# Retention feeding a SwiGLU block on one core: later retention with a row half per head, sequence and token half, 24 groups of small matmuls in place of 36, and a new order of steps

## The chip, the core and the metric

The kernel runs on one core of one Trainium2 chip. The metric is the device time in microseconds of that core, from launch to end. The kernel before takes 642.07 us (median of 3 runs, 642.02 to 642.96); lower is better. Times from the profile come from one profiled execution with a span of 640.5 us from its first to its last instruction.

The engines go by these names: PE is TensorE (PEld is its weight load), DVE is VectorE, ACT is ScalarE, POOL is GpSimd, SP is SyncE, which only issues transfers here. Each engine works through its own queue in the order in which the program issues instructions.

## What is computed

Retention over 4 sequences, 8 heads, 768 tokens and head size 64, then a SwiGLU feed-forward block over the 3072 tokens, all in float32:

```python
gamma = 1.0 - 2.0 ** (-5.0 - np.arange(H))
for t in range(S):
    state = gamma[None, :, None, None] * state + np.einsum('bhd,bhe->bhde', k[:, :, t], v[:, :, t])
    y[:, :, t] = scale * np.einsum('bhd,bhde->bhe', q[:, :, t], state)
...
x = y.transpose(0, 2, 1, 3).reshape(B * S, H * D)          # 3072 x 512
g = x @ w_gate                                             # 512 x 1536
silu = g * (1.0 / (1.0 + np.exp(-g)))
return silu * (x @ w_val) @ w_out                          # 1536 x 512
```

The retention is done in chunks. Within a chunk, scores (keys against queries) are weighted by a decay mask and multiplied with the values; what earlier tokens left is kept in a 64 x 64 state per head, read by the queries (scaled by the decay), decayed once per chunk, and increased by keys (scaled) against values.

## The kernel before

**Segments.** The 3072 tokens are worked in four segments of 768: two sequences of 384 tokens each. The feed-forward block of a segment has an up stage (12 column blocks of the gate and value weights; in the later segments each is 7 products of 128 x 128 blocks, `product` at L1088) and a down stage (12 steps f, each with six token blocks of 128, `down` at L1157, called D{f}.{tok}; three matmuls of 128x512 each, into banks 0 to 5 of PSUM). Numbers are kept exact by splitting each operand into three parts (`near_a/b/c` and `far_a/b/c`, L991 to L1007); the parts of the hidden values are made by h{f}.0 (ACT), h{f}.1 and h{f}.2 (DVE, 128x768 each). In the first segment the down weights are split too: d{f}.0 (ACT), d{f}.1 (POOL, 128x512), d{f}.2 (DVE, 128x512).

**Mixed stages.** The retention of the next segment is worked inside the down stage of the one before, so there are three mixed stages, each with three chunk positions p of two sequences, in token halves z of 64. PE does it in small matmuls of 64 x 64 (`mm`, L789; each leaves two records in the trace), set between D steps. Per p the kernel before has four groups: `s` (scores of both halves, 32 matmuls, `scores_of` L799), `A` (values of half 0, the old state's part, and the state's growth: `mix_a`, up to 40), `B` (`mix_b`, 32) and `C` (`mix_c`, 24): 12 groups in a stage, 36 in all.

**What stands around the groups.** dec{p}.{i} (`decayed`, L809, DVE) multiplies scores out of PSUM by the mask; q{p}.{i} (`scale_q2`, L814) scales the queries in place, one 128x512 on DVE and one on POOL; k{p}.{i} (`scale_k2`, L818) scales keys, 8 instructions of 128x64 on ACT (one of the six on POOL); was{p}.{z} (`decay2`, L885) decays the state, 4 instructions of 128x128 on ACT; new{p}.{z} (`keep_state`, L890, DVE) adds the growth out of PSUM; y{p}.{z}{j} (`bring_y`, L1020) copies the outputs out of PSUM, 16 copies of 64x128 per p on ACT. Then sum{p}.{m} and x{p}.{n}.{k} (`sum_x`, `x_part`) on DVE and ACT make the split operands of the next up stage. Scores of the first p stand in banks 4 and 5, those of the other two in banks 6 and 7, where the outputs and the state's growth stand as well.

**Order.** The order of all this on every engine is written out by hand as the text `PLAN` (L51): one name after another, and each name issues its instructions when its turn comes. `at(t, key, ...)` only registers what a name does; where PLAN has the name, its time t has no effect. l{n} are the loads of keys, queries, values and keys by rows (`load_pair`, L775: one or two transfers per chunk), L{f} and W{f} the loads of the weights, e{tok} and its store the output.

## Time and profile before

| what | us |
|---|---|
| median of the runs shown | 642.07 |
| span of the profiled execution | 640.5 |
| first mixed stage, from 127 to 196: DVE busy, ACT busy, POOL busy | 63.8, 50.2, 26.7 of 69 |
| second mixed stage, from 283 to 350: DVE, ACT, POOL | 50.1, 46.3, 10.0 of 67 |
| third mixed stage, from 435 to 502: DVE, ACT, POOL | 52.9, 44.7, 10.2 of 67 |
| ACT: copies of the outputs (L1022), decay of the state (L888), scaling of the keys (L824) | 36.6, 19.1, 29.8 in all |
| granted TensorE clock in all 40 slices | 0.9 or more |

A line of a timeline is: start, duration, engine, line of the kernel, operation, written tile <- read tiles, shape, number of instructions, and in brackets the idle time before it. An instruction on DVE is shown for about 0.07 us longer than it keeps the next one from starting. A line of the chain of waits is: start, length, engine and line, number of instructions. The windows give the busy time of each engine within a stretch.

### The profile page before, as it was taken

The page shows a single profiled execution, that of the slowest core. Times are in us where ns is not written, and L with a number is a line of the kernel's source. Part 1 is how long each engine was busy: PE and PEld are TensorE (multiplying, and loading weights), DVE is VectorE, ACT ScalarE, POOL GpSimd, SP SyncE. Part 2 cuts the span into 40 slices and gives each one's busy share as a digit, 9 for nine tenths or more (in the row PEclk, how much of TensorE's full clock was granted, in tenths as well). Part 3 has the DMA queues.
Part 4 walks back from the last instruction along what each step waited for, and adds up shares of the span by engine and source line. Part 5 has one row for each costly group of instructions (what it writes and reads, how often), then busy time and mean ns, then how long its engine had stood idle before and what let it go on. Part 6 is the DMA issues. An engine that isn't in the chain of part 4 may idle for free.

```text
span 640.5 us, 14132 instructions
## 1 busy us (share of the span) xinstructions
PE 632.9 (99%) x5587; PEld 580.4 (91%) x5587; DVE 484.1 (76%) x715; ACT 394.3 (62%) x868; POOL 261.1 (41%) x172
## 2 busy tenths in 40 slices
PE   7999999999999999999999999999999999999997
PEld 6899999987779999997778999998777999999886
DVE  4998787899898887665797869575789866768361
ACT  4787797777865565566766555564785555654221
POOL 1534445544425866630003665550101666663000
PEclk9999999999999999999999999999999999999999
DMA  9899998798787445258765640457776444304564
GB/s 320 291 332 326 376 329 269 268 326 305 266 285 278 168 148 173 75 179 260 247 239 214 211 152 15 175 196 246 226 258 248 154 164 173 116 1 151 194 214 148
DMA packets 50626, 139.60 MB, mean 218 GB/s; under 512 B 5120, under 2 KB 18176, under 8 KB 50560
## 3 DMA queue, kind: packets, MB, share of 16 engines
q1 hardware_dynamic: 49984, 137.92, 62.6%
q8 instruction: 44, 0.72, 0.5%
q10 hardware_dynamic: 576, 0.79, 0.3%
q14 instruction: 22, 0.18, 0.1%
HBM read 108.80 MB, written 29.88 MB: 217 GB/s over the span
## 4 chain that ended last, share of the span: by engine, by line
PE 97%; DMA 3%; SPq 0%; DVE 0%; ACT 0%; issue 0%
PE bank L1088 41%; PE bank L1157 32%; PE bank L919 13%; PE bank L789 6%; PE bank L937 3%; DMA hT<-in_v_n_dram 2%; PE bank L744 1%; DMA hT<-in_q_t_dram 1%; PE bank L730 0%; PE bank L715 0%; PE bank L633 0%; DVE chunk_x L1178 0%; SPq L513 0%; ACT chunk_x L1180 0%; SPq L466 0%
## 5 line engine op out<-in xcount | busy, mean ns | idle before, releaser
L1157 PE MATMUL bank<-oitem,gitem 128*128 128x512 f32 x867 | 208.2, 394 | 0.0
L1157 PEld LDWEIGHTS bank<-oitem,gitem 128*128 128x128 f32 x867 | 159.6, 188 | 34.5 <-DVE tmp L812 0.4
L997 POOL TENSOR_TENSOR gitem<-gitem 128x768 fp32r<-128x768 f32 x71 | 138.7, 1963 | 117.9 <-DVE gitem L994 99.0
L1088 PE MATMUL bank<-xa,gitem 128*128 128x384 f32 x864 | 160.5, 334 | 0.0
L1088 PEld LDWEIGHTS bank<-xa,gitem 128*128 128x128 f32 x864 | 150.8, 188 | 0.2
L997 POOL TENSOR_TENSOR oitem<-oitem 128x256 fp32r<-128x256 f32 (+1 forms) x60 | 64.1, 1074 | 56.8 <-DVE oitem L994 48.3
L1088 PE MATMUL bank<-xb,gitem 128*128 128x384 f32 x432 | 84.5, 334 | 0.0
L919 PE MATMUL bank<-xa,oitem 128*128 128x384 f32 x480 | 84.3, 335 | 0.0
L919 PEld LDWEIGHTS bank<-xa,oitem 128*128 128x128 f32 x480 | 83.0, 188 | 0.4 <-ACT tmp L444 0.2
L994 DVE SCALAR_TENSOR_TENSOR gitem<-gitem,loads 128x768 fp32r<-128x768 f32 x72 | 75.1, 1057 | 9.1 <-ACT gitem L991 7.5
L1088 PEld LDWEIGHTS bank<-xb,gitem 128*128 128x128 f32 x432 | 75.9, 188 | 0.4
L991 ACT ACTIVATE gitem<-loads 128x768 fp32r<-128x768 f32 x72 | 59.6, 843 | 26.0 <-PE bank L1088 16.8
L994 DVE SCALAR_TENSOR_TENSOR gitem<-gitem,hT 128x768 fp32r<-128x768 f32 x48 | 46.1, 965 | 24.4 <-ACT gitem L991 24.4
L991 ACT ACTIVATE gitem<-hT 128x768 fp32r<-128x768 f32 x48 | 40.2, 842 | 31.4 <-PE bank L1157 29.4
L1022 ACT COPY chunk_x<-bank 64x128 f32<-64x128 f32 x144 | 36.6, 260 | 32.6 <-PE bank L789 21.3
L401 DVE SCALAR_TENSOR_TENSOR gitem<-gitem 128x768 fp32r<-128x768 f32 x49 | 49.7, 1022 | 1.3 <-DVE gitem L994 0.5
L816 POOL TENSOR_TENSOR loads<-loads,tab 128x512 f32<-128x512 f32 x9 | 13.4, 1493 | 82.1 <-PE bank L789 44.6
L1088 PE MATMUL bank<-xb,oitem 128*128 128x384 f32 x216 | 43.4, 335 | 0.0
L1088 PEld LDWEIGHTS bank<-xb,oitem 128*128 128x128 f32 x216 | 37.9, 188 | 0.3
L994 DVE SCALAR_TENSOR_TENSOR oitem<-oitem,loads 128x256 fp32r<-128x256 f32 (+1 forms) x42 | 34.5, 824 | 2.1 <-ACT oitem L991 2.1
L1105 DVE TENSOR_TENSOR hT<-bank,tmp 128x384 f32<-128x384 f32 x36 | 20.0, 555 | 20.7 <-PE bank L1088 20.4
L1103 ACT COPY tmp<-bank 128x384 f32<-128x384 f32 x36 | 17.2, 478 | 28.3 <-PE bank L1088 19.3
(118 smaller groups left out, 789.8 us busy)
## 6 DMA issues: line engine op xcount, KB each, us to landing
loads<-wup SPq DMA_DIRECT2D x36, 896.0 KB, 4.7
oitem<-wdnt SPq DMA_DIRECT2D x33, 768.0 KB, 4.4
wdnt<-oitem SPq DMA_DIRECT2D x12, 768.0 KB, 5.5
wup<-first SPq DMA_DIRECT2D x9, 896.0 KB, 6.7
rawp<-in_w_gate_dram SPq DMA_DIRECT2D x12, 512.0 KB, 6.8
rawp<-in_w_val_dram SPq DMA_DIRECT2D x12, 512.0 KB, 6.2
rawp<-in_w_out_dram SPq DMA_DIRECT2D x12, 512.0 KB, 5.7
out_dram<-chunk_x SPq DMA_DIRECT2D x21, 256.0 KB, 2.1
```

What stands on the lines that cost most here:

```text
L401: stt(o, x, 1.0, y, op0=mul, op1=op)
L789: nc.tensor.matmul(o, a, b, start=start, stop=True, skip_group_check=True)
L919: nc.tensor.matmul(o, w[:, a, ts(b, P)], X0[:, a, i, NC - 1 - b], start=a == b == 0, stop=a == 2 and b == NC - 1, skip_group_check=True)
L937: nc.tensor.matmul(o, w[:, a, ts(b, P)], X0[:, a, :, NC - 1 - b, ts(j, P)], start=a == b == 0, stop=a == 2 and b == NC - 1, skip_group_che ...
L991: act(o[0], x, AF.Copy, scale=CUT / FAR)
L994: stt(o[1], f32(o[0]), -FAR, x, op0=mul, op1=add)
L997: op(o[2], f32(o[0]), f32(o[1]), op=add)
L1022: copy(cx[half[i], ds(2 * h, 2), c, half[z]], y.rearrange("p (b t) -> p b t", b=2))
L1088: nc.tensor.matmul(o, w[:, a, k], x[:, a, KH - 1 - k], start=start and a == k == 0, stop=a == 2 and k == KH - 1, skip_group_check=True)
L1103: steps = (lambda: copy(p1, x), lambda: tt(c11, z, p1, op=add), lambda: act(gate, c11, AF.Silu, scale=ONE), lambda: copy(u2, x), lambda: c ...
L1105: lambda: copy(p5, wb), lambda: tt(h1, x, p5, op=add),
L1157: nc.tensor.matmul(banks[tok][:, cols], hs[f][:, a, ds(i * TH + u * P, P)], wo[f][:, a, cols], start=f == a == 0, stop=f == NF - 1 and a = ...
```

## The change

**What it does.** The retention of the three mixed stages is laid out anew. The work is still 128 small matmuls per p, but the 128 rows of SBUF are assigned otherwise: a row half (64 partitions) belongs to a head pair, a sequence and a token half, by `row(z, c, g)`. With this the old state's part of both sequences can be worked together, and per p there are three groups (`s`, `A`, `B`), the last two by `mix2`. In PLAN the scores of the second p stand directly behind `A` of the first, so that a stage has 8 changeovers from D steps to small matmuls, and the three stages 24 (36 before).

**Banks.** The scores of the first and the second p stand in banks 4 and 5, those of the third in 6 and 7; D0.4 and D0.5 come behind `sc1`.

**What stands around the groups.** Scores are weighted by four DVE instructions per p (two of 128x384, two of 128x128). The queries are scaled by eight instructions of 64 partitions x 256 per p, four on DVE and four on POOL, and are written into the buffer of the keys, behind the scores that read it. The state is decayed by four instructions of 64 x 256 per p and z, all on POOL (`WAS_POOL`). Keys are scaled on ACT alone: 4 instructions of 128x128 and 8 of 128x64 per p. Outputs are copied by 4 instructions of 128x256 per p on ACT. Before the first mixed stage's parts, eight copies (`turn_state`, cv) put the state into the new layout.

**Loads.** Values and keys by rows come in four transfers of 64 partitions x 2 x 256 elements per pair (three before). Two pairs have new places (`chunk_x`, `tmp` and `last`). The first three loads of the first mixed stage, which were P2, P1 and P0 within the first up stage, come later, next to l3. The output's store is a step of its own, o{tok}.

**Order.** PLAN is written anew from the end of the first up stage on. PE's order in the second mixed stage, before and after (sc, A, B, C without their stage, p11.n and p0.n are products of the up stages):

```
-sc0 D0.0 p11.6 D0.2 D0.1 D0.4 D0.3 D1.0 D1.1 D0.5 A0 D1.5 D1.3 D2.1 B0 D1.2 D1.4 D2.5 D2.0 D2.3 D2.2 C0 ...
+sc0 p9.4 ... p11.6 D0.0 D0.1 D0.2 D0.3 A0 sc1 D1.0 D1.1 D1.2 D0.4 D0.5 D1.3 D1.5 D1.4 B0 D2.0 ... D3.1 A1
+D3.2 ... D4.3 B1 D4.5 ... D5.4 sc2 D6.0 ... D7.1 A2 D7.2 ... D8.3 B2 D8.4 ... D11.5 p0.0
```

In the first mixed stage W11:1 (the last product of the first up stage) is followed by sc0, D0.0 to D1.1, A0, sc1, and so on; ten D steps stand from D11.0 on to the next up stage. Two parts of PLAN there, with the names of DVE and POOL among PE's:

```
+    0/D4.5 1/y1.11 1/new1.1 0/d6.0 1/was2.03 0/D4.4 1/L0 0/h7.0 0/d6.1 0/D5.0 0/W7 1/y1.10 0/D5.1
+    0/h7.1 0/h8.0 1/was2.02 0/D5.2 1/x1.2.0 0/d6.2 1/was2.00 1/x1.1.0 0/D5.3 0/h7.2 0/Z6 1/was2.01 0/D5.4
...
+    1/sum2.0 0/Z10 0/d11.0 1/sum2.1 0/D9.5 1/w0.0.1 0/d11.1 0/D9.4 1/sum2.2 1/w0.1.0 0/D10.0 1/sum2.3 1/x2.0.0
+    0/d11.2 0/D10.1 1/w0.0.2 0/Z11 0/D11.0 1/w0.2.0 1/x2.1.2 0/D11.1 1/x2.1.1 0/D10.2 1/w0.1.1 0/e0 0/D11.2
```

In the up stages the products of one column block now follow each other in order (p5.0 to p5.6, then p6.0), where before two blocks were interleaved. The code, cut to its core (the removed functions are shown above):

```diff
+LATE = [(0.1, 'g4'), (14.2, 'g5'), (33.6, 'L'), (47.2, 'h0'), (47.2, 'h1'), (47.6, 'k4'), (53.1, 'k5'), (53.2, 'h2'), (56.3, 't4 t5')]
...
+    spots += [chunk_x[:, ts(i, 512)] for i in (2, 3)] + [tmp[:, ts(2, 512)], last]
+    HOME = (2, 3, 4, 5, 0, 1, 3, 6, 1, 4, 5, 0)
     blocks = [loads[:, ds(i, UNIT)] for i in (2048, 2048 + UNIT, 0)]
...
+    lmask = [local[:, ds(k * NP * HC, NP * HC)].rearrange("p (i n) -> p i n", i=2)
+             for k in range(2)]
+    lk, lg = (local[:, ds(2 * NP * HC + k * H, H)] for k in range(2))
+    lk = lk.rearrange("p (k n) -> p k n", k=2)
...
+    def row(z, c, g):
+
+        return g ^ (c & z & 1)
+
     def local_k():
 
         for m in range(2):
...
+            for k in range(2):
+                nc.sync.dma_start(out=lk[half[m], k],
+                                  in_=decays[half[1], ds(KDEC0 + NP * (k ^ m), NP)])
+        nc.sync.dma_start(out=lg, in_=decays[ds(D - 1, 1), ds(KDEC0, H)].to_broadcast([P, H]))
...
+            if w < 2:
+                nc.sync.dma_start(out=own[c], in_=src)
+                continue
+            for r in range(2):
+                step = D * DM + (c and 256 * (1 - 2 * r))
+                nc.sync.dma_start(out=two_of(own[c][half[r]]),
+                                  in_=bass.AP(src.tensor, src.offset + 256 * r,
+                                              [[DM, D], [step, 2], [1, 256]]))
...
     def scores_of(p, own):
...
+        scored[p] = own
         kt, qt = ([pairs(t) for t in given[p][w]] for w in range(2))
+        for z in range(2):
+            for b in range(2):
+                for c in range(2):
+                    for g in range(2):
+                        for i in range(2):
+                            mm(banks[own + i][half[row(z, c, g)], ds(256 * c + 128 * z + HC * b, HC)],
+                               kt[c][half[i], 2 * g + b, half[z]],
+                               qt[c][half[i], 2 * g + b, half[z]], z == b == c == 0)
+
+    def decayed(p, i, k):
+        if (p, i) not in att:
+            att[p, i] = (tmp if p % 2 else spare)[:, ts(i, 512)]
+        src = banks[scored[p] + i]
+        if k:
+            tt(att[p, i][:, 384:], src[:, 384:], lmask[1][:, i], op=mul)
+        else:
+            o, x = (t[:, :384].rearrange("p (a n) -> p a n", a=3) for t in (att[p, i], src))
+            tt(o, x, lmask[0][:, i][:, None, :].to_broadcast([P, 3, 128]), op=mul)
+
+    def scale_q2(p, c, i, r, op):
+
+        o = given[p][0][c][half[r], ts(i, 256)]
+        q, d = (pairs(t)[half[i]] if t is not qdec else t[half[i]]
+                for t in (given[p][1][c], qdec))
+        if c == 0:
+            op(o.rearrange("p (b t) -> p b t", b=2), q[:, ds(2 * r, 2)], d[:, ds(2 * r, 2)], op=mul)
+            return
+        x = []
+        for t in (q, d):
+            x.append(bass.AP(t.tensor, t.offset + HC * r, [list(t.ap[0]), [256 + HC * (1 - 2 * r), 2],
+                                                          [P, 2], [1, HC]]))
+        op(o.rearrange("p (g b t) -> p g b t", g=2, b=2), *x, op=mul)
+
+    def q_of(p, z, c, g, b, i):
+        r = row(z, c, g)
+        at = 256 * i + (256 // 2 * b + HC * z if c == 0 else 128 * g + HC * b)
+        return given[p][0][c][half[r], ds(at, HC)]
+
+    def scale_k2(p, c):
+        kd = given[p][3][c].rearrange("p (z n d) -> p z n d", z=2, n=NP)
         for n in range(NP):
...
+            if c == 0:
+                act(kd[:, :, n], kd[:, :, n], AF.Copy, scale=lk[:, 0, ds(n, 1)])
+            else:
+                for z in range(2):
+                    act(kd[:, z, n], kd[:, z, n], AF.Copy, scale=lk[:, z, ds(n, 1)])
...
+    def state_of2(z, c, g):
+
+        return states[half[row(z + 1, c, g)], z, row(z, c, g)]
+
+    def turn_state(i, g):
+
+        for c in range(2):
+            copy(state_of2(1, c, g).rearrange("p (b i) e -> p b i e", b=2)[:, :, i],
+                 states[half[i], 0, c, ds(2 * g, 2)])
+
+    def y_at(z, c, g, b, i):
+        return banks[R0 + row(z, c, g)][half[i], ds(256 * z + 128 * (g if z else c) + HC * b, HC)]
 
     def low(p, z):
...
+        for b in range(2):
+            for c in range(2):
+                for i in range(2):
                     for r in range(2):
...
+                        g = row(z, c, r)
+                        mm(y_at(z, c, g, b, i),
+                           given[p][2][c][half[r], ds(256 * z + D * (2 * b + i), D)],
+                           att[p, i][half[r], ds(256 * c + 128 * z + HC * b, HC)], b == c == 0)
+
+    def old(p, z):
         for b in range(2):
...
+            for c in range(2):
+                for i in range(2):
+                    for r in range(2):
+                        g = row(z, c, r)
+                        mm(y_at(z, c, g, b, i), state_of2(1 - z, c, g)[:, 2 * b + i],
+                           q_of(p, z, c, g, b, i))
 
     def grow(p, z):
         for n in range(NP):
...
+            for c in range(2):
+                for g in range(2):
+                    r, own = row(z, c, g), ds(256 * z + D * n, D)
+                    mm(banks[R0 + r][half[row(z + 1, c, g)], ds(256 * (1 - z) + D * n, D)],
+                       given[p][3][c][half[r], own], given[p][2][c][half[r], own])
+
+    def mix2(s, p, z):
+        low(p, z)
+        if has_old(s, p, z):
+            old(p, z)
+        if has_new(s, p, z):
+            grow(p, z)
+
+    def decay2(z, c, g, op):
+        r = row(z, c, g)
+        op(state_of2(z, c, g), state_of2(1 - z, c, g),
+           lg[half[r], ds(NP * g, NP)][:, :, None].to_broadcast([D, NP, D]), op=mul)
 
     def keep_state(s, p, z):
         for r in range(2):
...
+            new, st = states[:, z, r], banks[R0 + r][:, ds(256 * (1 - z), 256)]
+            st = st.rearrange("p (n e) -> p n e", n=NP)
             if has_old(s, p, z):
...
+    def bring_y(z, r):
+        y = banks[R0 + r][:, ts(z, 256)].rearrange("p (w b t) -> p w b t", w=2, b=2)
+        at, step = (HC + P * r, 512 + P * (1 - 2 * r)) if z else (512 * r, P)
+        copy(bass.AP(chunk_x.tensor, chunk_x.offset + at,
+                     [list(chunk_x.ap[0]), [step, 2], [256, 2], [1, HC]]), y)
...
+    def store(s, tok):
+        if (s, tok) in stored:
+            to, t = stored.pop((s, tok))
+            nc.sync.dma_start(out=to, in_=t)
...
+    Q_POOL, WAS_POOL = (1, 2, 5, 6), (0, 1, 2, 3)
...
+            for p in range(L):
+                at(t, f"{nxt}/sc{p}", scores_of, p, 6 if p == 2 else 4)
+                for i in range(4):
+                    at(t, f"{nxt}/dec{p}.{i}", decayed, p, i % 2, i // 2)
+                for i in range(8):
+                    at(t, f"{nxt}/q{p}.{i}", scale_q2, p, i // 4, i // 2 % 2, i % 2,
+                       pool if i in Q_POOL else tt)
+                for c in range(2):
+                    at(t, f"{nxt}/k{p}.{c}", scale_k2, p, c)
+                for z in range(2):
+                    at(t, f"{nxt}/{'AB'[z]}{p}", mix2, nxt, p, z)
+                    if has_new(nxt, p, z):
+                        for i in range(4 if has_old(nxt, p, z) else 0):
+                            at(t, f"{nxt}/was{p}.{z}{i}", decay2, z, i // 2, i % 2,
+                               pool if i in WAS_POOL else tt)
+                        at(t, f"{nxt}/new{p}.{z}", keep_state, nxt, p, z)
+                    for r in range(2):
+                        at(t, f"{nxt}/y{p}.{z}{r}", bring_y, z, r)
+                make_x(t, nxt, p, table)
```

More of the change, by code (lines that the diff above doesn't have):

```diff
@@ L224 @@
[L224 to L228 removed]
+    A0 I0 l0:0 l1:0 A2 A1 U0:0 s0 a0:1 r1 l0:2 s1 b0:1
@@ L1239, in down_stage @@
                 at(t + WHEN["end" if nxt else "last"][tok], f"{s}/e{tok}", finish, s, tok)
+                at(t + WHEN["end" if nxt else "last"][tok], f"{s}/o{tok}", store, s, tok)
         for f in range(NF):
@@ L1276, in tile_retnet_swiglu @@
     end = T0 + (NF - NPF) * UP0
-    for n in range(3, 5):
-        at(end + 0.1 + 0.01 * n, f"1/l{n}", load_pair, 1, n)
     t = down_stage(0, end)
@@ L1285, in tile_retnet_swiglu @@
         t += NF * UPT
-        if s + 1 < NSEG:
-            for n in range(5):
-                at(t - (18, 13, 12, 5, 4)[n], f"{s + 1}/l{n}", load_pair, s + 1, n)
         t = down_stage(s, t)
```

502 lines of the change are left out of this document (199 added, 303 removed).

## The prediction

> **What bounds the kernel now.** I read the chain of waits first: who sets the end.
>
> ```profile
> PE 97%; DMA 3%; SPq 0%; DVE 0%; ACT 0%; issue 0%
> ```
>
> From 18 us on PE waits for nobody. Whatever the change moves between ACT, DVE and POOL gains nothing by itself; only PE time counts, or a wait where there was none. So next, the chain in order of time, for what a group of small matmuls costs PE.
>
> ```profile
> 185.48 0.39 PE bank L789 x16
> 185.87 10.43 PE bank L1157 x45
> ...
> 291.64 2.27 PE bank L1157 x9
> 293.91 0.86 PE bank L789 x48
> 294.77 4.31 PE bank L1157 x18
> ...
> 305.61 1.09 PE bank L789 x64
> ```
>
> Two straight lines lie in these rows. Down matmuls: 45 take 10.43 and 9 take 2.27, so 0.2267 each (0.68 for a D step of three) and 0.23 over for each piece behind a group. Small matmuls: 64 records take 1.09 and 16 take 0.39, so 0.0146 each (0.0148 with the other rows) and 0.15 over. One changeover to small matmuls and back costs 0.15 + 0.23 = 0.38 us, besides the records.
>
> Then how near DVE and POOL are to becoming the bound. The tightest place is the first mixed stage, where DVE also splits the down weights: from the end of j11:1 (133.07) to the end of d11.2 (190.26), for which D11.1, at 191.5 by counting 7 D steps back from 196.30, waits.
>
> ```profile
> 133.07:190.26 57.19, 57.19 (x861) 45.15 (x860) 53.21 (x75) 43.85 (x126) 20.76 (x14) 1.00 0.84 293
> ```
>
> The columns behind the length are PE, PEld, DVE, ACT and POOL: DVE is busy 53.2 of 57.2. Why so much, the timelines of DVE and POOL show.
>
> ```profile
> 134.19 0.95 DVE L994 SCALAR_TENSOR_TENSOR gitem<-gitem,hT 128x768 fp32r<-128x768 f32 x1
> ...
> 138.34 1.50 DVE L401 SCALAR_TENSOR_TENSOR first<-first 128x256 f32<-128x256 f32 x1
> ...
> 142.10 0.41 DVE L401 SCALAR_TENSOR_TENSOR first<-first 128x256 f32<-128x256 f32 x1
> ...
> 163.04 1.42 DVE L994 SCALAR_TENSOR_TENSOR gitem<-gitem,hT 128x768 fp32r<-128x768 f32 x1 [1.47 <-ACT gitem L991]
> ```
>
> ```profile
> 138.14 1.42 POOL L1003 TENSOR_TENSOR oitem<-oitem 128x512 fp32r<-128x512 f32 x1 [4.43 <-ACT oitem L1000]
> ...
> 162.35 1.30 POOL L1003 TENSOR_TENSOR oitem<-oitem 128x512 fp32r<-128x512 f32 x1 [3.51 <-ACT oitem L1000]
> ...
> 216.28 0.73 POOL L997 TENSOR_TENSOR oitem<-oitem 128x256 fp32r<-128x256 f32 x1
> ```
>
> The same DVE instruction takes 0.41 alone and 1.50 when POOL has just begun: it ends 0.28 behind POOL's end (139.56). At 163.04 a 128x768 takes 1.42, not 0.95, and ends 0.81 behind POOL's. DVE instructions with two SBUF operands stand still while POOL works, for its whole instruction; in this stage I found none of them running through a POOL instruction that was itself running. So the two take turns, and their times add.
>
> Count the turns in that stretch. DVE by the distance of starts: 0.86 for 768 columns (134.19 to 135.05), 0.61 for 512, 0.34 for 256, 1.14 for 1024. Before: 21 x 0.86 + 17 x 0.61 + 16 x 0.34 + 4 x 1.14 = 38.4. POOL: 14 instructions of 128x512 at 1.30 = 18.2. Together 56.6 of 57.2. The turns are full; the slack before D11.1 is 191.5 - 190.26 = 1.2 us.
>
> **The change, part by part.**
>
> Groups: 36 become 24, the 256 records per p stay. 12 x 0.38 = 4.6 us saved, if no group waits: 1.5 per stage. The order of row halves within `grow` differs, but before, `grow` already had equal row halves side by side at the same 0.0148; cost 0.
>
> ACT: copies of outputs 36 instead of 144 (36 x 0.38 = 13.5 for 36.6), no state decay (-19.1), key scaling 9 x (4 x 0.39 + 8 x 0.34) = 38.5 for 29.8, cv 8 x 0.26 = 2.1: about 31 us less. ACT isn't on the chain: 0. Were PE to wait for a copy, it would be some tenths per p.
>
> Loads: 18 more transfers on SP and a later start of the first three. SP's queue isn't waited for; landing takes 4.5 to 5.4 us and they stand some nine PE us ahead of sc0 (nine W and G products of 1.04). I take 0; late behind the weight loads they would cost up to 3 us once. Stores as steps of their own, the small tables: 0.
>
> Up stages: products in order, each turn of a bank has one product (1.04 us) to hide one 0.48 us copy; ACT has time: 0. If the copy comes late, 0.1 per block, 3 us in all.
>
> DVE: per p four masks (2 x 0.47 + 2 x 0.20, PSUM operand) for two of 0.61, and four q of 0.34 for one of 0.61: 0.9 us more, of which 0.75 are turns.
>
> POOL: here is the price. Per p four q and up to eight state decays of 64x256. No row has a 64-partition instruction on POOL. From above, the 128x256 row: 0.73. From below, half of it, 0.37. I take 0.73: on ACT a 64x512 copy takes 0.62 (L769), a 128x512 one 0.60 to 0.63, so half the partitions save nothing. Per stage 12 q and 20 decays, 32 x 0.73 = 23.4, in place of 4 x 1.30 = 5.2: 18 us more turns.
>
> New waits: q is written into the keys' buffer, so it waits for PE's scores; behind it stand d1.1 on POOL and the masks on DVE, for which A and D1.0 wait. In the later stages sc0 comes 10 us ahead, so 0 there. D0.4 and D0.5 wait for the masks of sc1: PE has 0.23 + two or three D (1.6 to 2.3 us) before them, the masks take 1.34 and in the first stage a state add of 0.7 stands ahead: 0 to 1 us, within the waits that follow.
>
> First stage, the same stretch (j11:1 to d11.2 in the new PLAN): DVE 20 x 0.86 + 15 x 0.61 + 28 x 0.34 + 4 x 1.14 = 40.4. POOL 11 splits x 1.30 + 12 q x 0.73 + 17 decays x 0.73 = 35.5. Sum 75.9. PE from the end of W11:1 to D11.0: 62 D x 0.68 + 736 records x 0.0148 + 8 x 0.38 = 56.1; j11:1 ends 0.67 behind W11:1. So D11.0 waits until 76.6: 20.5 us of waits, spread over D3.0 to D11.0 wherever d{f}.2 or h{f}.2 is late. Ten D steps (6.8) then lead to p0.0: 83.4 behind W11:1, against 63.9 before (132.40 to 196.30): +19.5. No cover hides this: it is the bound.
>
> The Trainium skill has a rule here (SBUF — State Buffer, Who interferes with whom): a DVE instruction with two SBUF inputs and a GpSimd instruction that reads SBUF exclude each other for the whole instruction. By that rule, the trace agrees (0.41 against 1.50). A mean of rows would say otherwise: POOL's 18.2 us cost DVE only about 7, as DVE was at PSUM operands or idle during the rest; at that rate 35.5 would cost 14, DVE 48 + 14 = 62 and D11.0 some 6 us. I take the turns, because the hidden part (7.3 us of masks and state adds) doesn't grow.
>
> Second and third stage: DVE 50.1 and POOL 10.0 busy of 67, some 10 of it at PSUM: turns 50 at most. New: 50 + 18 + 2 - 4 (q of the first p, moved into the up stage) = 66 of 67 - 1.5. Full, as the first stage was before, but unevenly: between B1 and A2 the state decay, x1, q2 and then the masks stand in line, and behind B2 three POOL decays meet the first weight splits. Between 0 and 8 us of waits each; I take 2.5, as the first stage before ran full without any.
>
> Sum: +19.5 (its 1.5 saved is in it) + 2 x (2.5 - 1.5) = +21.5. The profiled execution has a span of 640.5, the median is 642.07, so 1.6 lies around it; 642.1 + 21.5 = 663.6, said as 663.
>
> **The rivals.**
>
> Turns taken, half price: a 64-partition POOL instruction holds 0.37. First stage 40.4 + 14.3 + 29 x 0.37 = 65.4, D11.0 late by 10, p0.0 by 9; the others free, -3. 642 + 6 = 648. For it: no row excludes it; against: the ACT rows.
>
> Pile-up in all three: 8 us of waits in the second and third too: 19.5 + 2 x 6.5 = 32.5, 675. For it: PE's groups are fixed points between which turns can't be shifted; against: the last two stages have nothing to split on POOL.
>
> Faster: half-row instructions on POOL don't stop DVE at all. One mechanism, at D3.0 to D11.0 of the first stage: DVE alone needs 40.4 + 14.3 + 0.7 = 55.4 of 56.1, so it decides from a hold under 0.03 us per instruction. Then the 4.6 stay: 637.5. For it: POOL is idle by the page (41%) and PE loses its changeovers for certain; against: every POOL form in the trace stops DVE.
>
> The mean rate above, 4.5 less than the 6: about 643, no change or a little slower.
>
> **How the numbers follow.** Turns at full price 0.60, half price 0.15, pile-up 0.12, no stop 0.09, mean rate 0.04. 0.2% (1.3 us) is what a measurement of this kernel can tell. Faster 0.09, same 0.03, slower 0.88. The range reaches from 644, under half price, to 678, over pile-up: what lies outside is faster, mean rate and some tails, under 0.2.
>
> **What would show it.** In the first mixed stage PE has idle time before L1157, released by DVE's writes of oitem (d{f}.2) or gitem (h{f}.2); PE's share in the slices of 127 to 215 us falls under 9; POOL is busy over 35 us there, with new 64x256 forms at 0.7 or more, and DVE's 256 and 768 forms have a mean well over 0.41 and 0.95. The chain has DVE and POOL in it. Changeovers: rows of 96 and 160 records with 0.15 over. Wrong, if PE still sets 97% of the chain: then DVE ran beside POOL; or if the waits sit before L789, for loads or copies.

## The result and the profile after

| | before | after |
|---|---|---|
| median, same chip (7 runs each), us | 643.02 (642.02 to 644.55) | 687.04 (681.85 to 688.30) |
| ratio, 95% interval | | 1.0667 (1.0640 to 1.0695) |
| span of the profiled execution, us | 640.5 | 680.1 |
| from the last W11:1 matmul to p0.0 of the second segment | 64.0 | 89.2 |
| up stage 2, to its last product | 89.3 | 93.0 |
| second mixed and third up stage | 151.3 | 160.0 |
| third mixed and fourth up stage | 152.3 | 154.4 |
| last down stage | 51.7 | 53.2 |

The kernel became slower, by more than the prediction's range allowed (663, 644 to 678). The stage lengths are read from the first and last matmul of each kind; the profiled execution of after is the 681.85, the fastest of the seven; the other six, at 684.42 to 688.30, have no profile, so where they lose the rest isn't shown.

The slices of the page of after, PE's busy share and the granted clock, and the first line of the chain:

```profile
PE   8999999978898899999999799999999889999997
...
PEclk9999999988978999999999799999999999999999
...
PE 74%; DVE 11%; DMA 8%; issue 3%; ACT 2%; SPq 1%; POOL 1%; ACTq 0%; DVEq 0%; POOLq 0%
```

PE no longer sets 97% of the chain but 74%. PE's busy share is under 9 in most slices from 136 to 238 us and in a few later ones. The granted clock, which never fell below 9 before, has 8 or 7 in four of the five slices from 136 to 221 us, and a 7 at 374. The PE waits in that stretch (line waited at, released by what: us, times, longest):

```profile
PE bank L1197 <- DVE oitem L1045: 7.9, 4, 2.3
PE bank L1197 <- ACT oitem L1038: 3.3, 1, 3.3
PE bank L1197 <- POOL oitem L1041: 1.6, 2, 0.9
PE bank L812 <- issue: 1.5, 1, 1.5
```

L1197 is `down` (L1157 before), L812 `mm`, L1045, L1038 and L1041 are the three steps of the down weights' split d{f}.2, d{f}.0, d{f}.1. So it is the split that is late: d{f}.2, as forecast, but d{f}.0 and d{f}.1 as well; and see what stands ahead of it. The chain of waits of after in the same stretch, in order of time:

```profile
136.30 1.42 DVE loads L853
...
137.74 0.86 DVE loads L853
138.60 0.87 DVE loads L847
...
139.49 0.56 DVE tab L839
140.05 0.61 DVE oitem L1045
...
140.70 1.59 PE bank L1197 x4
142.29 3.60 PE bank L812 x156
145.90 1.53 issue
...
163.97 2.13 PE bank L812 x96
...
171.76 1.56 PE bank L812 x96
...
179.49 7.55 DMA oitem<-wdn
...
187.13 0.64 ACT oitem L1038
...
191.40 9.28 DMA oitem<-wdn
```

Three things stand here beside each other. The query scalings (L853, L847) and a mask (L839) stand ahead of d1.2 on DVE: turns. Two loads of down weights land 7.55 and 9.28 us after their issue and set the chain: late loads. And the matmuls run slow: four D matmuls take 1.59 where four took 0.91 at 0.2267 each, 156 small ones 3.60 where 0.15 + 156 x 0.0147 gives 2.44. The row of 96 at 1.56 is as forecast, 0.15 + 96 x 0.0147; the one at 163.97 took 2.13, in a stretch (160 to 165) whose granted clock was 0.68.

The windows (length; busy PE, PEld, DVE, ACT, POOL with counts; granted clock; DMA share; GB/s): first the stage of before as a whole, then that of after and the pieces where the clock fell.

```profile
131.90:195.90 64.00, 64.00 (x890) 50.87 (x890) 58.95 (x83) 47.54 (x134) 21.93 (x15) 1.00 0.86 306
```

```profile
130.20:219.50 89.30, 74.96 (x956) 58.05 (x955) 80.08 (x107) 35.41 (x78) 51.34 (x46) 0.89 0.72 243
...
135.00:140.00 5.00, 3.77 (x11) 2.60 (x9) 4.97 (x8) 0.00 (x0) 4.73 (x5) 0.71 1.02 400
140.00:145.00 5.00, 4.30 (x116) 3.56 (x120) 3.24 (x7) 0.00 (x0) 0.06 (x1) 0.66 1.03 270
...
190.00:195.00 5.00, 5.00 (x102) 4.04 (x102) 5.00 (x8) 0.89 (x3) 1.82 (x2) 0.50 0.69 161
```

PE is idle for 14.3 of 89.3 us; it is busy for 75.0, where its work at the full clock is 62.9 (72 D steps of 0.68, 736 records, 8 changeovers). So by this estimate 12 us of the stage are slow matmuls, not waits. Before, PE's work in the same stretch comes to as much: 63.1 with 672 records (64 stand ahead of it) and 11 changeovers. From 135 to 140, DVE and POOL are both full (4.97 and 4.73 of 5), and the DMA share is 1.02. PE's timeline there, the first waits of the stage:

```profile
134.15 4.61 PE L1197 MATMUL bank<-oitem,gitem 128*128 128x512 f32 x12 [1.66 <-DVE oitem L1045]
140.70 1.59 PE L1197 MATMUL bank<-oitem,gitem 128*128 128x512 f32 x4 [1.93 <-DVE oitem L1045]
```

Twelve D matmuls take 4.61, where 12 at 0.2267 are 2.72.

### The profile page after: what moved, and what is told of

Read it like the earlier page. It is cut to its first block, busy times and chain, and to the rows that moved or that the text cites. A ratio compares the mean times of both kernels' runs of the same rounds, so it can differ in the third digit from the quotient of the medians.

```text
span 680.1 us, 14225 instructions
## 1 busy us (share of the span) xinstructions
PE 645.9 (95%) x5587; PEld 588.9 (87%) x5587; DVE 539.5 (79%) x760; ACT 358.5 (53%) x697; POOL 341.9 (50%) x256
## 4 chain that ended last, share of the span: by engine, by line
PE 74%; DVE 11%; DMA 8%; issue 3%; ACT 2%; SPq 1%; POOL 1%; ACTq 0%; DVEq 0%; POOLq 0%
PE bank L1128 35%; PE bank L1197 23%; PE bank L957 11%; PE bank L812 5%; DMA oitem<-wdn 2%; DMA rawp<-in_w_out_dram 2%; DVE gitem L1032 2%; DVE loads L853 1%; DVE loads L847 1%; DMA oitem<-wdnt 1%; DVE tmp L409 1%; DVE oitem L1032 1%; DVE oitem L1045 1%; DMA hT<-in_k_t_dram 1%; DMA hT<-in_q_t_dram 1%
## 5 line engine op out<-in xcount | busy, mean ns | idle before, releaser
L1197 PE MATMUL bank<-oitem,gitem 128*128 128x512 f32 x867 | 212.4, 402 | 13.6 <-DVE oitem L1045 7.9
L1197 PEld LDWEIGHTS bank<-oitem,gitem 128*128 128x128 f32 x867 | 163.9, 192 | 52.7 <-DVE oitem L1045 10.2
L1035 POOL TENSOR_TENSOR gitem<-gitem 128x768 fp32r<-128x768 f32 x71 | 153.3, 2172 | 97.6 <-DVE gitem L1032 90.2
L1128 PE MATMUL bank<-xa,gitem 128*128 128x384 f32 x864 | 158.3, 336 | 3.3 <-ACT tmp L1145 3.3
L924 POOL TENSOR_TENSOR states<-states,local 64x256 f32<-64x256 f32 x60 | 50.0, 834 | 65.1 <-DVE states L932 46.2
L1128 PE MATMUL bank<-xb,gitem 128*128 128x384 f32 x432 | 82.2, 336 | 0.3 <-DVE xb L409 0.3
L1032 DVE SCALAR_TENSOR_TENSOR gitem<-gitem,hT 128x768 fp32r<-128x768 f32 x48 | 48.3, 1006 | 16.9 <-ACT gitem L1029 16.8
L1128 PE MATMUL bank<-xb,oitem 128*128 128x384 f32 x216 | 45.4, 346 | 7.5 <-DVE hT L1145 7.5
L1061 ACT COPY chunk_x<-bank 128x256 f32<-128x256 f32 x36 | 12.5, 372 | 62.6 <-DVE states L932 36.6
L1032 DVE SCALAR_TENSOR_TENSOR oitem<-oitem,loads 128x256 fp32r<-128x256 f32 (+1 forms) x42 | 40.6, 966 | 0.2
```

The costliest lines, as they stand in the source:

```text
L924: op(state_of2(z, c, g), state_of2(1 - z, c, g), lg[half[r], ds(NP * g, NP)][:, :, None].to_broadcast([D, NP, D]), op=mul)
L1032: stt(o[1], f32(o[0]), -FAR, x, op0=mul, op1=add)
L1035: op(o[2], f32(o[0]), f32(o[1]), op=add)
L1061: copy(bass.AP(chunk_x.tensor, chunk_x.offset + at, [list(chunk_x.ap[0]), [step, 2], [256, 2], [1, HC]]), y)
L1128: nc.tensor.matmul(o, w[:, a, k], x[:, a, KH - 1 - k], start=start and a == k == 0, stop=a == 2 and k == KH - 1, skip_group_check=True)
L1197: nc.tensor.matmul(banks[tok][:, cols], hs[f][:, a, ds(i * TH + u * P, P)], wo[f][:, a, cols], start=f == a == 0, stop=f == NF - 1 and a = ...
```

## The experiments

The kernels differ from the one named in the lines shown. "First stage" is the 64.0 of before and 89.2 of after. Times are medians of one round (two runs), ratios against before on the same chip. A stage length comes from one profiled execution. Kernels whose order is the same up to there (after, up_cover and up_cover_only; all_orders and all_orders_2) differ by 1 to 1.5 us in the first stage, so smaller differences show nothing.

| run | us | ratio (95%) | first stage |
|---|---|---|---|
| before_with_holds | 663.1 | 1.0315 (1.0285 to 1.0345) | 80.5 |
| short_pool | 673.0 | 1.0468 (1.0438 to 1.0499) | 82.9 |
| retention_all_dve | 695.6 | 1.0820 (1.0771 to 1.0869) | 90.7 |
| decay_act_query_dve | 694.8 | 1.0807 (1.0715 to 1.0900) | 84.3 |
| loads_behind_w | 684.6 | 1.0644 (1.0608 to 1.0681) | 88.1 |
| splits_first | 682.5 | 1.0612 (1.0581 to 1.0642) | 86.5 |
| short_pool_both_orders | 669.7 | 1.0412 (1.0369 to 1.0456) | 76.4 |
| all_orders_2 | 678.9 | 1.0546 (1.0487 to 1.0604) | 84.9 |
| best_mix | 680.1 | 1.0581 (1.0551 to 1.0612) | 84.0 |
| no_decay_no_query | 673.8 | 1.0466 (1.0405 to 1.0528) | 80.5 |
| no_decay_no_query_all_orders | 664.7 | 1.0325 (1.0230 to 1.0420) | 77.7 |
| split_burst | 661.5 | 1.0290 (1.0260 to 1.0320) | 74.9 |
| split_burst_no_stores | 663.8 | 1.0325 (1.0263 to 1.0388) | 73.7 |
| before_three_stalls | 659.7 | 1.0263 (1.0232 to 1.0293) | 64.0 |

**The price of POOL's work in the old order.** To the kernel before, holds were added that nothing waits for:

```diff
+    def hold(n):
+        for i in range(n):
+            t = warm[half[i % 2]]
+            pool(t, t, t, op=mul)
+
     def decay2(s, p, z):
+        hold(6)
...
         (pool if i else both)(t, t, qdec, op=mul)
+        if i:
+            hold(6)
```

> The kernel before, its order untouched, with 48 POOL instructions of 64x160 on a scratch tile added in each mixed stage (six behind each state decay and behind each POOL query scaling); nothing waits for them. At some 0.45 each they are 21 us of turns per stage. Theory of the turns: in the first mixed stage 56.6 + 21 against 57.2, so 20 us of PE waits there, 2 to 8 in each of the others: 666 to 685 in all. If only the new order makes the loss, or if POOL's 64-row instructions don't stop DVE: 642 to 646.

Measured: 20.2 slower, 16.5 of it in the first stage, 2.5 and 1.8 in the others with their up stages. The window of its first stage:

```profile
132.00:212.40 80.40, 70.00 (x890) 53.73 (x889) 63.38 (x84) 47.30 (x134) 50.41 (x58) 0.94 0.74 254
```

POOL went from 21.9 busy to 50.4 and the stage from 64.0 to 80.4. In sum, the price that the prediction put on POOL's work (+19.5 in this stage, +21.5 in all) is near, in the order for which it was worked out; the total lies just under the 666 to 685 expected here. In kind it isn't: 20 us of PE waits were expected, and PE is idle for 10.4 us; the other 6.0 are matmuls that take 70.0 and not 64.0, at a granted clock of 0.94. Whether DVE stands still or POOL's own work (the split d.1, a query scaling) is late behind the holds this run doesn't separate.

**The same work taken out of the new kernel.** First cut short on POOL (the diff shows the decays; POOL's query scalings likewise), then moved to other engines:

```diff
-        op(state_of2(z, c, g), state_of2(1 - z, c, g),
-           lg[half[r], ds(NP * g, NP)][:, :, None].to_broadcast([D, NP, D]), op=mul)
+        op(state_of2(z, c, g)[:, :, :1], state_of2(1 - z, c, g)[:, :, :1],
+           lg[half[r], ds(NP * g, NP)][:, :, None], op=mul)
```

> The kernel after, with the same order and the same waits, but POOL's state decays and POOL's part of the query scaling work on 64x4 elements and not 64x256 (so 63 of 64 of this work is left out). Theory of the turns (POOL's instructions hold DVE): the 32 holds per stage all but vanish, PE's 34 us of idle time and the low granted clock go with them; the first mixed stage is 64 to 67 us long and not 89, the third up stage 87 to 89 and not 97.5, in all 637 to 645 us. Theory of the order (products in order, weights and loads placed late in PLAN): the waits stay where they are, 665 us or more.

```diff
-    Q_POOL, WAS_POOL = (1, 2, 5, 6), (0, 1, 2, 3)
+    Q_POOL, WAS_POOL = (), ()
```

> The kernel after with all state decays and all query scalings on DVE, none on POOL. Theory of the turns: a POOL instruction of 64x256 took a turn of 0.64 (decay) or 0.83 (query); on DVE it takes about 0.38, so the first stage has 17 x 0.26 + 12 x 0.45 = 9.8 us less of turns, and DVE's PSUM work is less well hidden: the first mixed stage 78 to 82 us and not 89, in all 652 to 668. Theory of the order: no part of the waits goes, 680 or more, as DVE has more to do. If POOL's instructions cost DVE only a share of their time, DVE becomes the bound by itself: above 685.

```diff
+        for n in range(NP):
+            act(state_of2(z, c, g)[:, n], state_of2(1 - z, c, g)[:, n], AF.Copy,
+                scale=lg[half[r], ds(NP * g + n, 1)])
```

> The kernel after with the state decay on ACT (four activations of 64x64 for each of 64x256) and all query scalings on DVE. Theory of the turns: first stage 40.4 + 12 x 0.38 + 14.3 = 59.3 of turns against PE's 56.1, D11.0 late by about 3; in all 638 to 650. The ACT theory (decay on ACT delays copies and splits there, 21 us more of it per stage): 650 to 665 with waits released by ACT. Theory of the order: 670 or more.

The last of these kernels has the line of the one ahead of it as well. All three expectations of the theory of the turns failed: 82.9, 90.7 and 84.3 in the first stage, where 64 to 67, 78 to 82 and some 66 (three over PE's work) were to be expected. The 64x4 instructions are no clean removal: the decays among them still have a mean of 438 ns in this stage, and the shortest takes 192. But with nothing of the retention on POOL the kernel is slower still. In decay_act_query_dve the first stage gains 4.9, and the second mixed with its up stage loses 9 (169.0, where ACT is busy for 106.0 and not 81.4). In retention_all_dve no stage gains: the first is 90.7, although DVE's 64x256 take 0.42 and POOL's 0.61 or more. It ends at 695.6, the outcome that was expected (above 685) if POOL's instructions cost DVE only a share of their time. So in the new order the full price of a turn isn't shown by these runs. That DVE and POOL hold each other up is seen again in the query scalings on DVE, first of after, then of retention_all_dve (count, busy us, mean ns):

```profile
L853 DVE TENSOR_TENSOR loads<-loads,tab 64x256 f32<-64x256 f32 x18 | 16.9, 939 | 0.3
```

```profile
L853 DVE TENSOR_TENSOR loads<-loads,tab 64x256 f32<-64x256 f32 x36 | 18.6, 517 | 0.7
```

The same form takes 939 beside POOL's decays and query scalings and 517 without. So the turns are real and yet don't set the stage alone. What is left to try is the order.

**The order.** Loads and splits, each alone and both:

```diff
-    ... 1/L0 0/D5.0 0/W7 ... 1/L1 0/Z7 0/D7.1 0/W9 ... 0/W11 0/Z9 0/D9.0 1/L2 ...
+    ... 0/D5.0 0/W7 ... 0/Z7 0/D7.1 0/W9 1/L0 ... 0/W11 1/L1 1/L2 0/Z9 0/D9.0 ...
```

> The kernel after with three names of the order moved: L0 behind W9, L1 and L2 behind W11 in the first mixed stage, as they stood before; so the 256 KB loads of the down weights W7, W9 and W11 don't queue behind the 896 KB loads of the next up stage. Theory of the late loads: W7 and W9 landed 7.6 and 9.3 us after their issue, one PE wait of 3.3 us and the low clock behind it (0.50 in 190 to 195) are theirs; the first mixed stage goes from 89.2 to 80 to 84 us, in all 673 to 679. Theory of the turns (POOL's holds fill DVE whatever the loads do): less than 2 us gained, 679 to 685.

```diff
-    T10:0 ... T10:1 ... T10:2 W11:0 ... T9:2 Z10 ... Z9 ... Z17 1/begin ... 1/sc0 ... 0/d1.0 0/D0.0 1/q0.0 ... 0/d1.1 ... 0/d1.2
+    W11:0 ... 0/d1.0 0/d1.1 1/sc0 j11:1 0/d1.2 ... 0/D0.0 1/dec0.1 ... 1/dec0.3 1/q0.0 ... 1/A0 T10:0 ... Z17 1/begin
```

> The kernel after with the start of the first mixed stage in another order on DVE, POOL and ACT: the sums T9:2 and T10 of the last up weights and their stores behind A0, the split d1 ahead of the query scalings, the masks ahead of the query scalings. PE's order is untouched. Theory of the late start: PE's waits of 1.7, 1.9 and 1.5 us at 132 to 147 and the clock of 0.66 to 0.71 behind them (3 us) go, the first mixed stage is 4 to 8 us shorter, 674 to 679 in all. Theory of the turns: the work only moves, the waits come later in the stage: less than 2 us gained.

> Both changes of order (loads behind W, splits first) on the kernel with POOL's decays and query scalings cut to 64x4 elements (that part of the work is left out), which had 82.9 us in the first mixed stage. If the order of loads and splits is what holds that stage once POOL's holds are gone, it falls to 64 to 70 us and the whole to 654 to 661 from 673. If something else of the new layout holds it (more work on DVE, copies, products in order), it stays above 76 and the whole above 666.

Neither alone moves the whole beyond what runs of after differ by; the first stage gains 1.1 (within what equal orders differ by) and 2.7. Together, and with POOL cut short, it falls from 82.9 to 76.4, by more than the two gains together: there are several waits, and taking one away uncovers the next. It isn't the 64 to 70 that was expected if loads and splits held the stage; above 76 was expected if something else of the new layout does.

The waits in the up stages:

```diff
-    2/p0.3 2/u0.3 ... 2/u0.2 ... 2/p0.4 2/u0.4 ... 2/p0.6 ... 2/w3.2.0 ... 2/p1.0
+    2/p0.3 2/u0.3 ... 2/p0.4 2/u0.4 2/u0.2 ... 2/p1.0 2/p0.6 2/w3.2.0
```

> The kernel after with three places of the order changed in each of the three later up stages: product p0.6 behind p1.0, product p10.6 behind p11.0, and on ACT the gate u0.2 behind the copy u0.4; so at the two crowded places a product of the other block covers the copy, and the copy no longer stands behind a gate that waits for DVE. Theory of the lost cover (products in order): PE's waits of 1.7, 1.3, 3.3 and 0.7, and 1.0 us at 228, 304, 384 to 387 and 464 go for the most part, and the clock of 0.50 at 385 to 390 with them; the up stages lose 6 to 11 us, 671 to 677 in all. Theory of the turns: DVE is late there whatever PE's order, the waits move to the next product: less than 3 us gained, 679 or more.

> The kernel after with all three changes of order at once: loads behind W, splits first, and the cover in the up stages. POOL's holds are untouched. If the holds set the first mixed stage, it stays at 83 to 87 us whatever the order and the whole at 668 to 676; if order is the cause, the first stage falls under 76 and the whole under 662.

> All three changes of order, and the 64x256 instructions taken off POOL: the query scalings on DVE, half of the state decays on DVE and half on ACT (four activations of 64x64 each). Work of DVE in the first mixed stage by the shortest duration of each form: 58.6 + 12 x 0.38 + 10 x 0.34 = 66.6, POOL 15.8, of which some 9 at PSUM can overlap: 73 us of turns against 63 of PE. Theory of the turns with the order mended: the first mixed stage 72 to 77 us, the whole 648 to 658. If ACT (40 + 12 us there) or PE's clock holds it: 660 to 670.

In these three, w3.2.0 still stood ahead of p0.6 and wrote the slot that p0.6 reads, so p0.6 of each later segment used other weights and waited for them; up_cover (681.3) and all_orders (677.5) are replaced by the two that follow. best_mix is read for its first stage alone, which lies ahead of that: 84.0, not 72 to 77. DVE was busy 78.7 of 84.0 there.

> The kernel after with the cover in the up stages alone (p0.6 behind p1.0, p10.6 behind p11.0, the gate u0.2 behind the copy u0.4), and w3.2.0 behind p0.6, so that the slot which p0.6 reads isn't written before. Theory of the lost cover: the waits at 228, 304, 384 to 387 and 464 (8 us) go for the most part, 671 to 677 in all. Theory of the sum: DVE and POOL are behind there, the wait moves to the next product that needs a copy; less than 3 us gained.

> All three changes of order on the kernel after, w3.2.0 behind p0.6 here too; POOL's decays and query scalings in full. Theory of the sum: the work is the same 95 us, so the first mixed stage stays at 82 to 87 and the whole at 664 to 674. Theory of the order: under 76 and under 660.

up_cover_only gave 681.9 in one run (the other, at 3538, is five times as long and isn't used) and a span of 680.1, as after: the wait of 3.3 at 384 became one of 3.8 at 389, before the moved p0.6 and for DVE. So these three changes of the products' order gain nothing; with DVE late, the wait moves on. All orders together bring 84.9 in the first stage and 678.9.

**Without the work.** Decays and query scalings left out on every engine, so that DVE and POOL have what they had before. Counted by the shortest duration of each form (on DVE less the 0.07 us that it is shown too long), the first stage then has 53.7 + 15.7 = 69.4 us of their work, before 51.7 + 17.6 = 69.3, after 58.6 + 36.7 = 95.3:

```diff
     def decay2(z, c, g, op):
+        return
...
     def scale_q2(p, c, i, r, op):
+        return
```

> The kernel after, its order untouched, without the state decays and without the query scalings on any engine (that work is left out). Work of DVE and POOL in the first mixed stage by the shortest duration of each form: 54.0 + 15.8 = 69.8, as in the kernel before (51.7 + 17.6 = 69.3 in 64.0 us), where the kernel after has 58.6 + 36.7 = 95.3 in 89.2. Theory of the sum (DVE and POOL work one after the other and their summed work sets the stage, wherever it is put): the first mixed stage 63 to 69 us, the whole 641 to 654. Theory of the order: the late loads and splits hold the stage at 75 us or more, the whole above 660.

> The same left out, with the three changes of order (loads behind W, splits first, cover in the up stages). Theory of the sum: 62 to 66 us in the first mixed stage, the whole 638 to 648; what this is below the run without the changes of order is the price of the order by itself. If the new groups of small matmuls cost PE more than counted, it stays above 650 with PE busy throughout.

The window of the first stage of no_decay_no_query:

```profile
131.60:212.10 80.50, 70.20 (x955) 54.38 (x954) 62.25 (x93) 35.55 (x78) 21.58 (x13) 0.94 0.77 268
```

Equal work of DVE and POOL, and 80.5 instead of 64.0: so the rest of the change (order, grouping, loads) costs 16.5 us in this stage by itself. PE is idle for 10.3 of the 80.5, and its matmuls take 70.2. The mended order brings 77.7. The timeline of PE in no_decay_no_query shows one cause that no theory had:

```profile
138.64 0.69 PE L812 MATMUL bank<-tab,loads 64*64 64x64 f32 x32
139.15 0.65 PE L812 MATMUL bank<-loads,states 64*64 64x64 f32 x32
139.62 0.65 PE L812 MATMUL bank<-loads,chunk_x 64*64 64x64 f32 x32
140.09 1.11 PE L812 MATMUL bank<-loads 64*64 64x64 f32 x60
146.22 0.48 PE L812 MATMUL bank<-loads 64*64 64x64 f32 x4 [5.02 <-issue]
```

A0 (96 records) and sc1 (64) follow each other, and before the last two matmuls PE stands for 5.02 us without a releaser. In the records of the transfers, a block of 16 KB of instructions begins at 143.70 and takes 1.11; PE goes on 1.41 after its end. In after it is 1.53 at 145.90 with a block that ends at 145.89. In the nine runs with a wait of 1.2 to 5.0 us at this place, PE resumes 1.35 to 1.54 us after such a block ends; the DMA engines are full there (a share of 1.02 in after from 135 to 140, 1.04 in no_decay_no_query from 140 to 146). In four runs PE waits in the midst of the burst for query scalings (all_orders, all_orders_2, best_mix, splits_first), and there its end follows without this wait. In the third mixed stage of after the burst of 160 runs through, at a DMA share of 0.57 (475 to 480):

```profile
475.75 2.49 PE bank L812 x160
```

So, with all changes of order and without decays and query scalings, the burst was split, and in a second kernel the stores of the split weights were left out too:

```diff
-    1/A0 ... 1/sc1 ... 0/D1.2 ... 0/D1.3
+    1/A0 ... 0/D1.2 0/D1.3 1/sc1
```

> As the run without decays, without query scalings and with all changes of order (first mixed stage 77.7 us, a PE wait of 2.7 that nothing in the profile releases, between the 156th and the 157th record of the burst of A0 and sc1), with two more D steps moved between A0 and sc1, so that the burst of 160 records becomes 96 and 64. Theory of the instruction blocks (PE runs out of instructions there, as a block of 16 KB lands late while the DMA engines are full): the wait goes or falls under 1 us, the first stage is 74 to 76.5 us. If that wait has another cause it stays at 2 to 3 us or moves to the end of sc1.

```diff
-            at(t + z, f"{s}/Z{f}", lambda: nc.sync.dma_start(out=w_dn3[f], in_=wo[f].bitcast(U32)))
+            at(t + z, f"{s}/Z{f}", lambda: None)
```

> The same, and the twelve stores of the split down weights (768 KB each, Z0 to Z11) are left out too; the later stages load the unsplit weights three times instead, the same bytes. A slot of the ring of three isn't free for the next load W until its store has read it. Theory of the ring (W waits for the store, then lands late, then the split follows, and PE needs it): W lands in under 4 us, PE's waits for the split in 150 to 205 go, and the first stage falls to 64 to 69 us, PE's 63 and little more. If DVE's own work or something else holds it: 72 us or more.

The timeline of PE in split_burst at the same place:

```profile
139.58 0.65 PE L799 MATMUL bank<-loads,chunk_x 64*64 64x64 f32 x32
140.15 1.67 PE L1185 MATMUL bank<-oitem,gitem 128*128 128x512 f32 x6
141.75 1.36 PE L799 MATMUL bank<-loads 64*64 64x64 f32 x64
144.66 1.67 PE L1185 MATMUL bank<-oitem,gitem 128*128 128x512 f32 x6 [1.54 <-DVE tmp L826]
```

The wait is gone, and the stage is 74.9 as expected. A new wait of 1.54 stands behind sc1, for its masks on DVE, so the gain isn't the whole wait. The stores hardly count: 73.7, within what equal orders differ by, though the loads of the down weights land after 3.0 us (median) and not 4.1. The ring isn't what is left.

**The clock.** Stalls at three places of the kernel before:

```diff
+    STALL = {(1, 6): 8, (2, 6): 14, (3, 6): 24}
...
+        def first_copy():
+            for _ in range(many):
+                copy(warm, warm)
+            copy(p1, x)
```

> The kernel before with 8, 14 and 24 needless copies of 128x160 on ACT ahead of the first copy of block 6 in the second, third and fourth up stage, so that PE waits there some 1.5, 3.5 and 6.5 us. Theory of the clock: behind a long wait PE's granted clock is lowered for some us; each of the longer waits costs 2 to 3 us beyond itself, and the windows behind it show 0.5 to 0.7 (665 or less in all, 650 to 656). If the clock falls for other reasons (heat, the chip), it stays at 1.0 behind these waits and the kernel loses only the waits, some 10 to 12 us.

This run was not what it says: the count was shadowed by a later variable, so nine copies stood ahead of every block. It gave 703.0. The next one is as meant:

> The kernel before with 8, 14 and 24 needless copies of 128x160 (0.32 us each) on ACT ahead of the first copy of block 6 in the second, third and fourth up stage, and nowhere else; by the run with nine in every block these make PE wait about 1.2, 3.0 and 6.2 us. Theory of the clock: the first costs no more than itself, behind the others the granted clock falls to 0.5 to 0.7 for some 5 us and each costs 2 to 3 us beyond itself; 655 to 660 in all. If a wait alone doesn't lower the clock: the three waits and no more, 651 to 654.

Its PE timeline around the three waits:

```profile
245.07 3.39 PE L1088 MATMUL bank<-xa,gitem 128*128 128x384 f32 x18 [0.81 <-ACT tmp L1110]
...
400.09 3.66 PE L1088 MATMUL bank<-xa,gitem 128*128 128x384 f32 x12 [3.69 <-ACT tmp L1110]
...
404.64 2.24 PE L1088 MATMUL bank<-xa,gitem 128*128 128x384 f32 x12
...
559.92 3.92 PE L1088 MATMUL bank<-xa,gitem 128*128 128x384 f32 x12 [7.00 <-ACT tmp L1110]
```

Twelve matmuls take 2.24 at the full clock, 3.66 behind the wait of 3.69 and 3.92 behind that of 7.00; behind 0.81 nothing changes. The granted clock is 0.58 and 0.52 in the 3.4 us behind the two long waits (400.1 to 403.5, 560.1 to 563.5) and 1.00 in the 4.5 us after these. The stages with the waits are 1.2, 5.4 and 8.9 longer. By the matmuls a long wait costs 1.4 to 1.7 beyond itself, by the stage lengths 1.7 to 1.9; 2 to 3 was expected. The Trainium skill (TensorE: Matmul & The Clock Gate, Part 1: The HAM clock gate) says that PE's clock is halved after an idle window of about 3.4 us and given back after as much work; by these two waits, the trace agrees.

## Why the prediction was wrong

**Right.** Direction and place, and part of the mechanism: PE waits before `down` for d{f}.2 in the first mixed stage, and POOL is busy over 35 us there (51.3), its new forms at 0.61 (decays) and 0.73 (queries) at the shortest for the 0.73 taken. The clause "wrong if PE still sets 97%" didn't come true. One sign hardly came: DVE's 768 forms have a mean of 1.04 and 1.08 in this stage, where 1.00 and 1.07 stood before; only the split d{f}.2 went from 0.73 to 0.86. The changeovers came as forecast where the clock was full: rows of 96 at 1.56 and one of 160 at 2.49, 0.15 over; the burst of 160 in the first mixed stage broke. In the third mixed and fourth up stage PE's busy time fell from 152.3 to 150.1, but 1.4 of that are six D matmuls that now stand behind the last product: some 0.8 is left for the 1.5 forecast.

**Wrong.** The step that failed is the sum of the first stage, which let the larger of PE's work and the turns decide and put everything else of the new order at nothing: "Loads: ... I take 0; late behind the weight loads they would cost up to 3 us once". Equal DVE and POOL work in the new order takes 80.5, not 64.0. With the order's 16.5 already there, decays and queries add 8.7 to 89.2, not the 19.5 of the prediction; in the old order the like amount of POOL work adds 16.5. Each of the two alone costs 16.5, both together 25.2, 5.7 more than the sum had. That they fill the same waits, and part of one hides behind the other, is likely. Part of it is the wait for instructions alone, which is 5.02 without decays and queries and 1.53 in after.

That the price of the turns came near is in part luck. The sum put 20.5 us of waits in this stage; PE is idle for 14.3 in after and 10.4 in before_with_holds. Slow matmuls make up the rest, 12 and 6 us, and those it didn't have.

Of the order's part, the runs on the kernel without decays and queries show: loads, splits and cover 2.8 (80.5 to 77.7), the burst of 160 records 2.8 (to 74.9). The stores' 1.2 (to 73.7) is too little to tell. **Open:** the remaining 10.8 us against PE's 62.9, of which PE is idle for 6.4. Six waits of 0.2 to 1.9 us for d{f}.2 and one of 0.9 for d{f}.1 are left, and one of 1.55 for the masks of sc1; that the splits stand too close ahead of their D step is likely, but moving them all was not tried.

**Missing.** The clock has no term in the prediction. Over the profiled execution the mean granted clock went from 1.000 to 0.980, some 13.6 us of 680. PE's idle time in the mixed and up stages is 14.3 + 3.1 + 5.4 + 4.3 = 27.1 more than before, near the 25.5 of waits in the prediction's sum (20.5 and twice 2.5), though not where it put them: 12.8 lies behind the first stage and not 5. What the sum lacks beside is, in the profiled execution, for the larger part the lowered clock.

**Undersized.** "Up stages: products in order: 0" and 2.5 us of waits in each later stage: up stage 2 lost 3.7, the second mixed stage with its up stage 8.7, the third 2.1, the last 1.5. The last is no loss: 1.4 of it are the six D matmuls that stood in the third before, which so lost 3.5. By up_cover_only the products' order at the places tried isn't the cause. PE's waits before the products are for DVE (7.5 in all) and ACT (3.3), but the added work isn't the whole reason: with decays and queries left out, up stage 2 is still 95.0 long. The second is 157.3 then, 156.9 with the order mended and 153.3 in split_burst, whose order is the same in this stage; so single executions differ by some 3.6 here, and the cause in the later stages stays open.

**Rivals.** The pile-up (675) was nearest in time; of the 8 us of waits that it put in each of the later mixed stages, PE's idle time shows 5.4 and 4.3, with their up stages. Half price (0.37 for a 64-partition instruction on POOL) doesn't fit POOL's 0.61 at the shortest, but what such an instruction costs DVE in the new order wasn't settled (retention_all_dve). The faster case is out, and so is the mean rate as the whole of it: holds alone cost 3%. No version here beats the kernel before; the nearest with all of the work is all_orders_2, 5.5% behind.

## What to carry to other kernels

Price a new order by itself: with the work of each engine unchanged, how far ahead of its use does each load and each split still stand, and what big transfer now queues ahead of it. Two causes in one stage need not add (here 16.5 and 16.5 gave 25.2), so an experiment that removes one of them can understate it; remove both, and then put one back. Count a long PE wait with its tail, here 1.4 to 1.7 us of slow matmuls.

## What the runs showed of the hardware

- The clock also falls without a long wait: in after, behind waits of 1.66 at 132.5 and 1.93 at 138.8, the granted clock was 0.71 and 0.66 in 135 to 145, though neither reaches the 3.4 us named above. A single wait of 0.81 lowered nothing. No run here varies the shorter waits alone, so what rule they follow stays open.
- In the burst of 160 records of small matmuls in the first mixed stage PE waited 1.2 to 5.0 us before the last four of them, each time until 1.35 to 1.54 us after a block of instructions had landed. The Trainium skill (Runtime: NRT & Kernel Launch, Instruction fetch mechanics) calls the cost of crossing from one such block to the next mostly hidden; here it wasn't, and splitting the burst into 96 and 64 took the wait away. The burst of 160 in the third mixed stage, at a DMA share of 0.57, had no such wait; whether full DMA engines make the difference wasn't tried.
- Half rows save nothing on DVE, and little on POOL: 64x256 takes 0.42 on DVE, as 128x256 does (0.41); on POOL 0.61 (the shortest state decay) to 0.73 (the shortest query scaling) against 0.73. The new layout pays for twice the instructions.
